# Two attention and mixer layers on one core: the order in which the last V and the weights are loaded at a layer's end, and what PE does meanwhile

## The chip, the core and the metric

The kernel runs on one core of a Trainium2 chip. The metric is the device time of one execution in microseconds (us). Before the change it is 2575.71 us, the median of three runs (2574.78 to 2576.16). Times "at 1268" are microseconds from the start of the profiled execution's span.

## What is computed

A decode step of two layers for a batch of two rows of 576 values. Each layer does, in this order:

```
x = x + attention(layernorm(x)) @ wo        # 32 heads of 128, 16384 cached positions, per row
x = x + B(layernorm(x))                     # a mixer: h = gelu(layernorm(x) @ w1), shifted along
                                            # the sequence, @ w2; then gelu(layernorm(x1) @ w3) @ w4
attention: q = x @ wq;  p = softmax(q . K * 128**-0.5);  o = p @ V
```

Both layers use the same weights and the same K and V caches. One row's head (here a *unit*; there are 64, unit u is head u // 2 of row u % 2) has a K of 16384 x 128 bf16 values, 4096 KB, and a V of the same size. The sequence is one token long, so the shifted h is zero wherever it would be used, and w1 and w2 are loaded and multiplied all the same.

## The kernel before, in words

**What is where.** One SBUF array `mem` holds everything that is loaded: an area at its start (`AUX`, 6144 bytes of each partition), which during attention holds three buffers `kt` for transposed K, and behind it six slots of 32768 bytes, each as large as one K or V tile. `Store` (L250) keeps account of it. `plan_all` (L469) writes down by hand, in order, every load with its place: `plan_tile` for K and V, `plan_cols` for wq and w3 (128 rows of the matrix a piece, the last piece the remaining 64 rows), `plan_heads` for wo, `plan_groups` for w4, `plan_small` for w1 and w2. `Store.pump` (L271) issues the loads strictly in that order, all on SP's queue: a load is issued as soon as every cell of its place is free, and one whose place isn't free holds all those behind it. `used` and `release` free a place behind the instruction that reads it last.

**A step of attention** (`attention`, L859 and on). For each unit, half of K's blocks are transposed by PE in chunks of eight blocks (`transposes`, L1012) into a PSUM buffer `tps` (four of them), copied by ACT to `kt` (`evacuate`, L1022) and multiplied with q by PE (`scores`, L1032). The other half goes to DVE, as a product with a broadcast q and a sum (`dots`, L1047 and L1051, four pairs a unit). `softmax_max` (L1058 and on) takes maxima, with a GpSimd reduction over partitions; `softmax_exp` (L1073 and on) takes exponentials on ACT; `pv` (L1103) multiplies with V, one step later, in four quarters. So V of unit s is used in the step of unit s + 1.

**Order of the units.** Layer 0 goes from unit 0 to 63. Layer 1 begins with 62, 63, 61, 60, because the K of units 61 to 63 and the V of units 62 and 63 are still in their slots (`held`) and aren't loaded again; then it goes from 0 to 59. In layer 1 the two kept heads 62 and 63 have 40 instead of 32 of each half's 64 blocks transposed (`PB_KEPT`), and the first four chunks are transposed ahead of wq (`early_transposes`).

**The end of attention** (`last_head`). While the last unit's V is still to come, the sums of all other units are formed (`total`, L937), o is normalised, and wo is multiplied for all heads but the last (`heads_projection`, `rows_step`, L794). wo comes as head rows: for `a` to `b` heads, partition p of the piece gets row p of each head, 1152 bytes a run. In the plan, wo stands ahead of the last unit's V, which comes in four parts; in layer 0 wo's last pieces lie in AUX, which is free only when the last scores are done.

**Behind it**: `two_norms` gives the mixer's inputs, then w3 (`cols_projection`, L730 and L740), `gelu` (L828 to L833), w4 in eight groups (`groups_projection`, L794 again), the next layer's `input_norm`, and wq (`q_projection`). Weights of layer 0's end go into AUX and into slot 0, the only places that are free while five slots hold kept tiles; so a piece of w3 waits until a piece of wo has been multiplied, w4 until w3 has, wq until w4 has, and the next K tile until wq has. In layer 1 nothing is kept, and all weights find free slots.

Of the kernel before, what the change touches and what calls it, by code (L numbers as in the profile page):

```python
# [5 lines left out]
ALU = mybir.AluOpType  # L6
# [306 lines left out]
class KB:  # L313
# [12 lines left out]
    PB_KEPT = 40  # L326
    GROUPS = (6, 6, 6, 6, 6, 3, 2, 1)

    def __init__(self, nc, A_x, K, V, wq, wo, w1, w2, w3, w4, out):
# [20 lines left out]
        self.chunk = 0  # L350
# [4 lines left out]
    def _alloc(self):  # L355
# [21 lines left out]
        self.otn = sb("otn", [128, U], BF16)  # L377
        n = 2 * MT * B
# [3 lines left out]
        self.linv = self.prod[:, 512:512 + 2 * U].bitcast(FP32)  # L382
        self.linv_last = self.prod[:, 640:642].bitcast(FP32)
# [46 lines left out]
    def plan_cols(self, nm, l, w, ats):  # L430

        n = w.shape[1]
        for k, at in ats:
            if k < self.KT - 1:
                self.store.plan((nm, l, k), f"{nm}{k}", at, 2 * n, [(lambda m: m, w[k * 128:(k + 1) * 128, :])])
            else:
                self.store.plan((nm, l, k), f"{nm}{k}", at, n,
                                [(lambda m: m, w[k * 128:, :].rearrange("r (h n) -> (r h) n", h=2))])
        self.korder[nm, l] = [k for k, _ in ats]

    def plan_heads(self, l, cuts):

        D = self.D
        self.cuts["wo", l] = [(a, b) for a, b, _ in cuts]
        for i, (a, b, at) in enumerate(cuts):
            self.store.plan(("wo", l, i), f"wo{i}", at, 2 * (b - a) * D, [
                (lambda m: m.rearrange("p (j n) -> p j n", n=D),
                 self.wo[a * 128:b * 128, :].rearrange("(j p) n -> p j n", p=128))])
# [20 lines left out]
    def plan_all(self):  # L469
# [11 lines left out]
        for i, (t, u) in enumerate(tiles[:-1]):  # L481
            self.plan_tile(source[t], t, u, place[i])
            if i == 0:
                self.store.plan(None, "xin", 0, 0, [(self.rows[0:B, :], self.A_x.rearrange("b s d -> (b s) d"))], ["prod"])
                self.plan_cols("wq", 0, self.wq, [(k, s[0] + wqr * k) for k in range(self.KT)])
                self.plan_small("w2", 0, self.w2, s[0] + wqr * (self.KT - 1) + wqr // 2, (0, 64))
        at = s[0]
        self.plan_heads(0, [(0, 11, at), (11, 21, at + 11 * row), (21, 28, at + 21 * row), (28, 31, 0), (31, 32, 3 * row)])
        rest = self.store.queue[-2:]
        del self.store.queue[-2:]  # L490
        self.plan_tile(self.V, *tiles[-1], place[-1], 4)
        self.store.queue[-2:-2] = rest
        at = 4 * row
        self.plan_cols("w3", 0, self.w3, [(0, at), (1, at + w3r), (2, at + 2 * w3r), (4, at + 3 * w3r), (3, 0)])
        self.plan_groups(0, [w3r, w3r + g[0], w3r + g[0] + g[1], w3r + g[0] + g[1] + g[2], 0, g[4], g[4] + g[5],
                             g[4] + g[5] + g[6]])
# [696 lines left out]
```

## Time and profile before

| | |
|---|---|
| median of three runs | 2575.71 us |
| the profiled execution's own time | 2575.98 us |
| its span, first to last instruction | 2574.2 us |
| busy: PE, DVE, ACT, GpSimd | 63%, 73%, 47%, 6% |
| read from HBM | 1094.21 MB, 425 GB/s over the span |
| mean granted TensorE clock | 0.572 |

How to read it: the page's section 2 cuts the span in 40 equal slices of 64.4 us and gives each engine's busy tenths, the granted clock, the share of time in which the 16 DMA engines are busy, and GB/s. The stretches of the trace give the same for any window. In the chain, a line "DMA mem<-in_A_wo_dram" is the time from a transfer's issue to its landing, as far as something waited for it. A transfer's issue is an instruction of SP (SPq L98).

### The profile page before, as it was taken

The numbers are of one execution on the slowest core, as the hardware profiler recorded it, in microseconds if no ns is written. First come the engines' busy times: TensorE is split into PE (matmuls) and PEld (weight loads), VectorE is DVE, ScalarE is ACT, GpSimd is POOL, SyncE is SP. The second block draws the span as 40 slices with busy tenths as digits, with TensorE's granted clock in tenths as the row PEclk, the third lists the DMA queues.
The fourth block names the chain that finished last, engine by engine and source line by source line (L and its number), as shares of the span: only waits on it lengthen the run. The fifth ranks groups of instructions, "written<-read, shape, count | busy, mean of one in ns | idle before, by whom it ended". The sixth has DMA issues, their size and how long they took to land.

```text
span 2574.2 us, 73686 instructions
## 1 busy us (share of the span) xinstructions
PE 1623.4 (63%) x34362; PEld 1587.6 (62%) x34362; DVE 1889.8 (73%) x1905; ACT 1208.0 (47%) x1822; POOL 160.0 (6%) x151
## 2 busy tenths in 40 slices
PE   4766566666666656666667766666665665666565
PEld 3666566566656656666567766665665665666565
DVE  5877777776777777777549977777777777777773
ACT  3544444444544444454335554454444444445442
POOL 0000000000000000000000000000000000000000
PEclk8555655555555555555555655555555556555555
DMA  9999999999999999999999999999999999999998
GB/s 409 431 432 432 431 432 432 432 431 432 431 432 432 431 432 432 431 432 432 359 365 425 433 431 432 431 431 432 432 431 432 431 432 432 431 432 431 432 431 357
DMA packets 52143, 1095.27 MB, mean 425 GB/s; under 512 B 4954, under 2 KB 14558, under 8 KB 16862
## 3 DMA queue, kind: packets, MB, share of 16 engines
q1 hardware_dynamic: 52062, 1094.23, 99.4%
q8 instruction: 46, 0.75, 0.1%
q14 instruction: 35, 0.29, 0.0%
HBM read 1094.21 MB, written 0.00 MB: 425 GB/s over the span
## 4 chain that ended last, share of the span: by engine, by line
DMA 64%; DVE 28%; PE 5%; issue 1%; SPq 1%; ACT 0%; POOL 0%; another core or an unknown queue 0%; DVEq 0%; POOLq 0%
DMA mem<-in_A_k_cache_dram 61%; DVE s_dve L1051 17%; DVE prod L1047 9%; DMA mem<-in_B_w_dram 3%; PE tps L1012 2%; PE mps L1103 2%; SPq L98 1%; PE sps L974 1%; DMA mem<-in_A_wq_dram 0%; DMA mem<-in_A_wo_dram 0%; DVE diag L971 0%; DVE mx L1062 0%; DVE mx L1060 0%; DVE mx L1058 0%; PE sps L794 0%
## 5 line engine op out<-in xcount | busy, mean ns | idle before, releaser
L1022 ACT ACTIVATE mem<-tps 128x1024 bf16<-128x1024 bf16 x1028 | 1038.3, 1023 | 868.6 <-PE tps L1012 851.7
L1051 DVE TENSOR_REDUCE s_dve<-prod 128x16 f32<-128x2048 bf16 (+1 forms) x512 | 1166.1, 2278 | 17.5
L1012 PE MATMUL tps<-ident,mem 128*128 128x128 bf16 x8224 | 1004.9, 300 | 172.4 <-POOLq L177 171.0
L1047 DVE TENSOR_TENSOR prod<-mem,qb 128x2048 bf16<-128x2048 bf16 (+1 forms) x512 | 624.1, 1219 | 538.0 <-DMA mem<-in_A_k_cache_dram 520.6
L1103 PE MATMUL mps<-p,mem 128*128 128x1 bf16 x16384 | 515.6, 166 | 596.3 <-ACT p L1078 521.8
L1012 PEld LDWEIGHTS tps<-ident,mem 128*128 128x128 bf16 x8224 | 766.1, 136 | 181.8 <-POOLq L177 180.8
L1103 PEld LDWEIGHTS mps<-p,mem 128*128 128x128 bf16 x16384 | 487.7, 105 | 607.4 <-ACT p L1078 599.2
L1032 PEld LDWEIGHTS sps<-q_col,mem 128*128 128x128 bf16 x8224 | 413.2, 113 | 4.8 <-ACT mem L1022 4.7
L1032 PE MATMUL sps<-q_col,mem 128*128 128x1 bf16 x8224 | 401.5, 170 | 4.1 <-ACT mem L1022 4.1
L1065 POOL PARTITION_ALL_REDUCE mx<-mx x128 | 157.7, 1232 | 2358.8 <-DVE mx L1062 2358.8
L1073 ACT ACTIVATE mx<-mx 128x1 f32<-128x1 f32 x128 | 25.9, 203 | 325.9 <-POOL mx L1065 325.9
L974 PE MATMUL sps<-diag,ones_bf 128*128 128x128 bf16 x128 | 36.8, 288 | 119.6 <-DVE diag L971 119.6
L974 PEld LDWEIGHTS sps<-diag,ones_bf 128*128 128x128 bf16 x128 | 13.3, 104 | 130.4 <-DVE diag L971 130.4
L977 ACT ACTIVATE qb<-sps 128x128 bf16<-128x128 f32 x128 | 35.4, 277 | 75.2 <-PE sps L974 75.2
L1075 ACT ACTIVATE p<-s_dve,mx 128x64 bf16<-128x64 f32 x128 | 44.5, 348 | 4.2
L1078 ACT ACTIVATE p<-sps,mx 128x64 bf16<-128x64 f32 x128 | 37.5, 293 | 0.0
L1060 DVE TENSOR_REDUCE mx<-sps 128x1 f32<-128x64 f32 x128 | 27.4, 214 | 10.0 <-PE sps L1032 10.0
L559 ACT ACTIVATE sc<-sc 128x2 f32<-128x2 f32 x8 | 1.6, 204 | 65.5 <-DVE sc L556 65.5
L971 DVE TENSOR_SCALAR diag<-ident,q_f 128x128 bf16<-128x128 bf16 x128 | 31.3, 245 | 0.3 <-PE sps L974 0.3
L1058 DVE TENSOR_REDUCE mx<-s_dve 128x1 f32<-128x64 f32 x128 | 26.7, 208 | 0.1
L730 PE MATMUL sps<-xn,mem 128*128 128x2 bf16 x544 | 21.0, 174 | 9.1 <-DMA mem<-in_A_wq_dram 6.6
L730 PEld LDWEIGHTS sps<-xn,mem 128*128 128x128 bf16 x544 | 20.2, 122 | 9.6 <-DMA mem<-in_A_wq_dram 7.0
(96 smaller groups left out, 214.3 us busy)
## 6 DMA issues: line engine op xcount, KB each, us to landing
mem<-in_A_k_cache_dram SPq DMA_DIRECT2D x124, 4096.0 KB, 41.2
mem<-in_A_v_cache_dram SPq DMA_DIRECT2D x123, 4096.0 KB, 49.9
mem<-in_B_w_dram SPq DMA_DIRECT2D x8, 1152.0 KB, 15.7
mem<-in_B_w_dram SPq DMA_DIRECT2D x10, 864.0 KB, 17.7
mem<-in_A_wq_dram SPq DMA_DIRECT2D x8, 1024.0 KB, 12.4
mem<-in_A_v_cache_dram SPq DMA_DIRECT2D x8, 1024.0 KB, 10.7
mem<-in_A_k_cache_dram SPq DMA_DIRECT2D x2, 2048.0 KB, 9.2
mem<-in_A_v_cache_dram SPq DMA_DIRECT2D x2, 2048.0 KB, 9.6
```

Of the source, the lines that this page charges most:

```text
L730: ins = pe.matmul(out[:, m * B:(m + 1) * B], lhsT=buf[:, c:c + 127 * d + 1:d], rhs=self.xn[:, k, :], start=first and m == 0, stop=False, s ...
L974: self.pe(lambda pe: pe.matmul(qps, lhsT=self.ones_bf[:, :], rhs=self.diag[:, :], start=True, stop=True, skip_group_check=True), reads=["o ...
L977: self.act(lambda e: e.activation(out=self.qb[s % 2][:, :], in_=qps, func=ACT.Copy), reads=[("qps", i)], writes=[("qb", s % 2)])
L1012: ins = pe.transpose(self.tps[t][:, j * 128:(j + 1) * 128], buf[:, j * 128:(j + 1) * 128], self.ident[:, :])
L1022: self.act(lambda e: e.activation(out=self.kt[k], in_=self.tps[t][:, :].rearrange("p (i c) -> p i c", i=self.CH), func=ACT.Copy), reads=[( ...
L1032: ins = pe.matmul(self.sps[sp][:, c * self.CH + j:c * self.CH + j + 1], lhsT=self.kt[k][:, j, :], rhs=self.q_col[:, sp:sp + 1], start=True ...
L1047: self.dv(lambda e: e.tensor_tensor(out=prod, in0=buf.rearrange("p (j d) -> p j d", d=128), in1=qbc, op=ALU.mult), reads=[("qb", s % 2)] + ...
L1051: self.dv(lambda e: e.tensor_reduce(out=sd[:, c0:c0 + DB], in_=prod, axis=AX.X, op=ALU.add), reads=["prod"], writes=[("s_dve", s % 2)])
L1065: self.pool(lambda e: e.partition_all_reduce(self.mx[:, 3, m:m + 1], self.mx[:, 2, m:m + 1], channels=128, reduce_op=ROP.max), reads=[("mx ...
L1075: self.act(lambda e: e.activation(out=p[:, n:self.NB], in_=self.s_dve[s % 2][:, 0:self.NB - n], func=ACT.Exp, bias=self.mx[:, 4, m:m + 1], ...
L1078: self.act(lambda e: e.activation(out=p[:, 0:n], in_=self.sps[i][:, 0:n], func=ACT.Exp, bias=self.mx[:, 4, m:m + 1], scale=self.scale, acc ...
L1103: ins = pe.matmul(self.mps[:, 448:449], lhsT=buf[:, j * 128:(j + 1) * 128], rhs=p[:, col:col + 1], start=(h == 0 and b == 0), stop=(h == 1 ...
```

## The change

1. **Order of the loads.** In both layers the last unit's V is planned as one tile ahead of wo, in its turn as every other tile. In layer 1 the slots' ring is `[0, 5, 1, 2, 4, 3]` instead of `[0, 5, 2, 1, 4, 3]`, and the first tile (K of unit 60) comes in four parts, in the order 1, 2, 3, 0.
2. **wo's shape.** wo comes in five pieces: three of eight heads (1024 rows of the matrix), and the last eight heads cut in two. Partition p of such a piece gets the eight rows 8p to 8p + 7, one run of 9216 bytes. To match, o must lie so that partition p holds those rows' values: `dealt` multiplies the normalised o with eight selections of the identity's columns (`every`, copied by DVE), masks the product and sums it, for the first 48 units (`oA`) and later for the last 16 (`oB`). wo's pieces 0 to 2 use `oA`, the last eight heads `oB`; all are multiplied behind the last unit's PV.
3. **w3, w4, wq of layer 0's end** have new places in AUX and slot 0; w3's piece 3 comes in two halves; wq's order is 1, 2, 3, 4, 0.
4. **Both kept K** are transposed in full, in place: `ahead` has PE transpose a chunk into a `tps` buffer, `lay` has ACT copy it back to where it came from. Their 32 chunks are strewn between the sums, the pieces of wo, the norms, w3, w4 and wq. In layer 1 `kept_heads` scores units 62 and 63 straight from the transposed K, all 128 blocks on PE and none on DVE, both heads one after the other, before the loop over the other units begins.
5. **Small ones.** `touch` runs one-element activations to have a table loaded earlier; keys of the `prod` scratch are split.

The core of the diff:

```diff
     def plan_heads(self, l, ats):
+        cuts = [(i, 0, hg) for i in range(self.ng - 1)] + [(self.ng - 1, 0, self.WO_CUT), (self.ng - 1, self.WO_CUT, hg)]
+        for i, ((a, lo, hi), at) in enumerate(zip(cuts, ats)):
+            src = self.wo[a * hg * 128:(a + 1) * hg * 128, :].rearrange("(p j) n -> p (j n)", j=hg)
+            self.store.plan(("wo", l, i), f"wo{i}", at, 2 * (hi - lo) * D, [(lambda m: m, src[:, lo * D:hi * D])])
...
-        for i, (t, u) in enumerate(tiles[:-1]):
+        for i, (t, u) in enumerate(tiles):
             self.plan_tile(source[t], t, u, place[i])
...
-        self.plan_heads(0, [(0, 11, at), (11, 21, at + 11 * row), (21, 28, at + 21 * row), (28, 31, 0), (31, 32, 3 * row)])
-        self.plan_tile(self.V, *tiles[-1], place[-1], 4)
+        self.plan_heads(0, [a, a + r8, a + 2 * r8, 0, a + 3 * r8])
+        self.plan_cols("w3", 0, self.w3, [full(0, mt, a), full(1, mt, a + w3r), full(2, mt, a + 2 * w3r),
+                                          full(4, mt, a + 3 * w3r), (3, 0, mt // 2, 0), (3, mt // 2, mt, a)])
...
+    def ahead(self, l, n):
+        for _ in range(n):
...
+            nm, buf, keys = self.chunk_of(c)
+            def f(pe, buf=buf, t=t):
+                for j in range(self.CH):
+                    ins = pe.transpose(self.tps[t][:, j * 128:(j + 1) * 128], buf[:, j * 128:(j + 1) * 128],
+                                       self.ident[:, :])
...
+    def lay(self, l, n):
...
+            self.act(lambda e, buf=buf, t=t: e.activation(out=buf, in_=self.tps[t][:, :], func=ACT.Copy),
+                     reads=[("tps", t)], writes=keys)
...
+    def kept_heads(self, l, o):
+        for c in range(n):
+            self.kept_scores(l, 0, o[0], c)
+        self.softmax_max(l, 0, o[0])
+        while self.laid or self.made < 2 * n:
+            self.lay(0, 1)
+            self.ahead(0, 1)
+        for c in range(n):
+            self.kept_scores(l, 1, o[1], c)
+        self.softmax_exp(l, 0, o[0])
+        self.softmax_max(l, 1, o[1])
+        for g in range(4):
+            self.pv(l, 0, o[0], g)
+        self.keep_o(0, o[0])
+        self.softmax_exp(l, 1, o[1])
+        for g in range(4):
+            self.pv(l, 1, o[1], g)
...
     def last_head(self, l, s, u, before):
+        self.shares(0, late)
+        self.normed(0, late)
+        self.ahead(l, 2)
+        self.dealt(0, late, self.sps[2], ("sps", 2), self.masked[0], self.oA[:, :], "oA")
+        self.ahead(l, 2)
+        self.lay(l, 2)
+        self.softmax_exp(l, s, u)
+        self.touch(ACT.Sqrt)
+        self.lay(l, 2)
+        self.shares(late, U)
+        for g in range(4):
+            self.pv(l, s, u, g)
+        self.keep_o(s, u)
+        self.normed(late, U)
+        self.heads_projection(l, 0)
+        self.ahead(l, 1)
+        self.dealt(late, U, self.sps[0], ("sps", 0), self.masked[1], self.oB[:, :], "oB")
+        for i in range(1, len(self.cuts["wo", l])):
+            self.heads_projection(l, i)
+            if i < 3:
+                self.ahead(l, 2)
+                self.lay(l, 2)
+        self.lay(l, 4)
```

Further fillers (`ahead`) stand behind the statistics of `two_norms` (2) and of the next `input_norm` (2), ahead of w3's last half piece (3), behind each w4 group but the first (1 each) and behind each wq piece but the last (1 each).

More of the change, by code (lines that the diff above doesn't have):

```diff
@@ L325 @@
     PB = 32
-    PB_KEPT = 40
+    HG = 8
+    WO_CUT = 5
+    PK = ["prod", "gT", "hf", "every"]
     GROUPS = (6, 6, 6, 6, 6, 3, 2, 1)
@@ L745, in cols_projection @@
             first = False
+            if w == "w3" and i == len(order) - 2:
+                self.ahead(l, 3)
+                self.lay(l, 2)
+            if w == "wq" and i < len(order) - 1:
+                self.ahead(1 - l, 1)
+                self.lay(1 - l, 1)
     def q_projection(self, l):
@@ L941, in last_head @@
[L941 to L949 removed]
+        i, hg = self.ident[:, :], self.HG
```

339 lines of the change are left out of this document (201 added, 138 removed).

## The prediction

> **What bounds the kernel now.** I read the page's slices first, then its chain, then stretches of the trace around the turn from layer 0 to layer 1, then the chain in that stretch.
>
> ```profile
> span 2574.2 us, 73686 instructions
> PE   4766566666666656666667766666665665666565
> DMA  9999999999999999999999999999999999999998
> GB/s 409 431 432 432 431 432 432 432 431 432 431 432 432 431 432 432 431 432 432 359 365 425 433 431 432 431 431 432 432 431 432 431 432 432 431 432 431 432 431 357
> DMA 64%; DVE 28%; PE 5%; issue 1%; SPq 1%; ACT 0%; POOL 0%; another core or an unknown queue 0%; DVEq 0%; POOLq 0%
> ```
>
> The DMA engines are busy in every slice and move 431 to 433 GB/s in all but five: the first, three at the layer turn and the last. The kernel is a stream of bytes; only stretches in which the stream thins can be won back. One 4096 KB tile at 432 GB/s takes 9.71 us. Inside the turn (start:end, width, busy time of PE, PEld, DVE, ACT, POOL, granted clock, DMA share, GB/s):
>
> ```profile
> 120.00:1200.00 1080.00, 673.42 (x14151) 659.82 (x14149) 811.49 (x778) 513.67 (x777) 70.17 (x56) 0.57 1.00 432
> 1250.00:1260.00 10.00, 5.45 (x97) 5.37 (x96) 9.83 (x10) 6.05 (x10) 1.25 (x1) 0.67 0.77 273
> 1260.00:1270.00 10.00, 9.09 (x236) 8.90 (x234) 5.45 (x9) 5.29 (x9) 0.35 (x1) 0.50 1.04 383
> 1270.00:1280.00 10.00, 4.96 (x152) 4.80 (x150) 0.17 (x1) 0.00 (x0) 0.00 (x0) 0.50 0.56 194
> 1280.00:1290.00 10.00, 3.66 (x99) 3.22 (x96) 1.46 (x10) 0.06 (x1) 0.00 (x0) 0.50 1.01 426
> 1290.00:1300.00 10.00, 6.74 (x152) 6.66 (x153) 2.30 (x16) 0.35 (x2) 0.00 (x0) 0.50 0.77 288
> 1340.00:1350.00 10.00, 9.07 (x213) 8.99 (x211) 9.54 (x9) 6.21 (x11) 0.00 (x0) 0.50 0.63 236
> ```
>
> The stream thins where wo is issued (1250), where the queue runs dry behind wo (1270), behind w3 (1290), and at the first tiles of layer 1 (1340). The chain of waits, and then the issue of the transfers, say why (start, duration):
>
> ```profile
> 1245.08 15.85 SPq L98 DMA_DIRECT2D mem<-in_A_wo_dram  x2
> 1266.68 8.79 DMA mem<-in_A_wo_dram
> 1277.57 9.75 DMA mem<-in_B_w_dram
> 1287.46 0.28 PE sps L794 x5
> 1291.91 1.57 PE sps L730 x36
> 1293.50 5.61 DMA mem<-in_B_w_dram
> 1313.73 10.89 DMA mem<-in_A_wq_dram
> ```
>
> SP stands 15.85 us in issuing two wo pieces, and the last V waits behind them in SP's order. Three heads of wo wait for the kt buffers until 1266.68, the last head waits until those have landed, and half of the last V waits for that.
>
> **Before, in landings.** Each of these transfers is alone in a narrow stretch of the DMA view (KB, us from issue to landing): V of unit 62, issued at 1208.1; layer 1's K of unit 3, issued at 1401.9; V of unit 58, issued at 2470.99:
>
> ```profile
> mem<-in_A_v_cache_dram SPq DMA_DIRECT2D x1, 4096.0 KB, 51.0
> mem<-in_A_k_cache_dram SPq DMA_DIRECT2D x1, 4096.0 KB, 17.7
> mem<-in_A_v_cache_dram SPq DMA_DIRECT2D x1, 4096.0 KB, 51.1
> ```
>
> They land at 1259.1, 1419.6 and 2522.1. Between the first two come wo and wq (4.72 MB each), w3 and w4 (5.31 each) and ten tiles (41.9 MB): 62.0 MB, 143.5 us at 432 GB/s, where 160.5 passed. So 17 us can be won at the turn, and that is the ceiling.
>
> **The change, by a walk along the turn.** Durations for it (timeline; two pieces of the chain; three groups of the page):
>
> ```profile
> 1266.51 1.09 PE L937 MATMUL sps<-l,mean_f 128*128 128x63 f32 x4
> 1268.52 2.74 PE L794 MATMUL sps<-otn,mem 128*128 128x2 bf16 x97 [0.91 <-DVE otn L552]
> 1268.56 1.28 ACT L559 ACT_TABLE_LOAD   x1
> 1278.88 2.98 PE L1103 MATMUL mps<-p,mem 128*128 128x1 bf16 x96
> 1291.78 4.82 PE L730 MATMUL sps<-xn,mem 128*128 128x2 bf16 x108
> 1313.37 0.36 DVE L549 TENSOR_TENSOR st<-st,mps 128x8 f32<-128x8 f32 x2 [6.80 <-PE mps L794]
> 1313.98 0.62 PE L626 MATMUL mps<-st,mean_f 128*128 128x20 f32 x2 [0.65 <-DVE st L549]
> 1314.43 3.58 PE L1012 MATMUL tps<-ident,mem 128*128 128x128 bf16 x32
> 1317.81 0.24 PE L701 MATMUL mps<-xn,sel 128*128 128x2 bf16 x2
> 1258.64 0.44 ACT p L1075 x2
> 1259.08 0.30 ACT p L1078 x2
> L1022 ACT ACTIVATE mem<-tps 128x1024 bf16<-128x1024 bf16 x1028 | 1038.3, 1023 | 868.6 <-PE tps L1012 851.7
> L1051 DVE TENSOR_REDUCE s_dve<-prod 128x16 f32<-128x2048 bf16 (+1 forms) x512 | 1166.1, 2278 | 17.5
> L1047 DVE TENSOR_TENSOR prod<-mem,qb 128x2048 bf16<-128x2048 bf16 (+1 forms) x512 | 624.1, 1219 | 538.0 <-DMA mem<-in_A_k_cache_dram 520.6
> ```
>
> So a weight step of wo, w4 or wq costs 0.028 us a matmul (40 of them 1.15), one of w3 0.045 (36: 1.6), a filler of eight transposes 0.9 on PE and its copy back into K 1.02 on ACT, a quarter of PV 0.9.
>
> *1. V ahead of wo.* V63 now waits in SP's order for V60's slot only, freed one step (two tiles, 19.4 us) after the issue of V62: 1227.6, so wo behind it isn't held. It lands one tile after V62, at 1268.8, in one piece. wo follows from the other slot, where its issue was (1242.7 to 1247), in 9216-byte rows like w3's, so at 426 instead of 383 GB/s: 11.1 us, front at 1279.9. The queue has work throughout, and the 15.85 us of issuing goes, since a piece has 128 rows of one run instead of 1408.
>
> *2. First hand-over, w3's piece 0 into wo's piece 0.* PE: scores end 1266.5; sums 1.1; two fillers 1.8 (1269.4); eight dealing matmuls; two fillers (to 1271.8); sums again 1.0; PV of V63 3.5 (1276.3); 40 matmuls: w3 is issued at 1277.4. The trace shows no dealing matmul of 48 columns: between 8 x 0.028 = 0.2 and 8 x 0.11 (a transpose, 128 columns) = 0.9; I take 0.6, the nearer of them. DVE's copy of `every` (1024 elements, 0.6 to 1.2 by the rows of 2048), the masked product and its sum lie beside fillers and PV; uncovered they would cost some 2 us. On ACT two copies stand ahead of the last exponential and end at 1270.6; with 0.74 for the exponentials and 0.2 for the scale they still make PE's second sums at 1271.8.
>
> What an issue into a short queue costs is in the row of 1293.50: 5.61 us for 1152 KB, of which 2.8 at 426 GB/s, so 2.8 more. [...] Landing is then 1283.0 instead of 1282.7: **0.3 lost**. The next pieces are issued at 1280.2, 1283.1 and 1286.1 (each 1.15 behind one or two fillers, and once the dealing); the last of these is a 576 KB one, landing at 1286.1 + 2.8 + 1.4 = 1290.3 instead of 1289.9: **0.4 lost**. The front is at 1291.7 with all of w3 but its last 576 KB.
>
> *3. Second hand-over, w3's last half piece.* It needs piece 0 consumed. From the end of wo's matmuls to w3's first took 1287.74 to 1291.91 = 4.2; the fillers there sit beside DVE's norm. So 1286.1 + 4.2 + 1.6 = 1291.9, issue; landing 1291.9 + 2.8 + 1.4 = 1296.1 where a full queue had 1293.1: **3.0 lost**. w4 follows without a gap (pieces issued 1293.4, 1295, 1296; three fillers, 2.65, delay its fifth to 1300.4, still 5 us before its turn): 12.5 us, 1308.6. The sigmoid's table load of 1.28 leaves the path; that only hides fillers, as w4 is ahead.
>
> *4. Third hand-over, layer 1's first K into wq.* w4's eight steps end at 1313.3 with a filler each, as before (1313.37, the row of the x update), so the norm starts no earlier, though wq now lands at 1319.7 instead of 1313.73 + 10.89 = 1324.6. After the last w4 step PE runs a filler (0.9), the statistics (0.6), two fillers (1.8) and the spreading (0.24): wq's first step is at 1316.9, and the second is done at 1319.7 (0.9, a filler, 0.9): issue, landing of the 1024 KB at 1325.0 where a full queue had 1322.1: **2.9 lost**. The other three parts: 1332.4. wq is done at 1324.7.
>
> *5. Kept heads.* 128 score matmuls (3.5) free unit 62's slot at 1329.5; V61 lands at 1343.1, allowing 3.8 instead of 2.8 for a tile (**1.0 lost**). Five leftover fillers follow on PE, and ACT's five copies behind the first of them (1330.4) end at 1335.5, the second head's scores at 1337.4, its PV at 1344.5: two more slots, all earlier than their turn. DVE idles meanwhile and starts unit 61 at 1344.8; with four products of 1.22 + 2.28 a step takes 15.6, and each slot still comes free 1 to 5 us before its turn. K of unit 3 lands seven tiles after V61: 1411.1. **Gain 8.5.**
>
> *6. The end.* In layer 1 the order is V59, wo, w1, w3, w4, each into slots free some 10 us before. The last of it before:
>
> ```profile
> 2549.13 21.13 DMA mem<-in_B_w_dram
> 2570.31 0.67 PE mps L794 x15
> ```
>
> From 2522.1 to 2570.3 stands 48.2; V59 at 432 and wo, w3, w4 (15.34 MB) at 426 GB/s need 9.7 + 36.0 = 45.7. **Gain 2.5.** The tail behind the last w4 group, the start and the steady steps are as before; three GpSimd instructions more at the start lie under the first K.
>
> **Sum.** 8.5 + 2.5 = 11.0 from the profiled execution's 2575.98 us (span 2574.2 and 1.8 around it): 2565.0; the median stands 0.3 below that execution: **2564.7**. A difference under 0.2% (5.2 us) is about what a measurement can't tell from none.
>
> **Rivals.**
>
> *No thin places left (0.10).* The 7.6 us lost in steps 2 to 5 don't appear: 2557.1. What would do it is a faster PE on the filled stretch. The clock after a stretch full of transposes:
>
> ```profile
> 1329.90:1333.30 3.40, 3.40 (x53) 3.40 (x51) 3.30 (x4) 3.40 (x5) 0.00 (x0) 0.50 1.03 434
> 1333.30:1336.70 3.40, 2.27 (x60) 2.09 (x59) 3.33 (x3) 3.10 (x4) 0.00 (x0) 1.00 0.99 414
> ```
>
> Full clock was granted there. If it held from 1270 on, each filler would cost half (0.45), PE would be 4 us early at step 3 and more at step 4. Against it stands the row of 1260, 91% busy with PV and transposes mixed and granted 0.50; the new stretch is such a mixture. [...]
>
> *The gain is handed back (0.14).* The front's lead is worth something only if PE keeps pace, and steps 3 and 4 show that the chain is no earlier than before. If each of the four hand-overs is 2 us later than I walked it (semaphore steps, the deal at 0.9, ACT's queue), 8 more go: 2572.7, within 0.2%.
>
> *Slower (0.08): ACT sets the fillers' pace.* Four transpose buffers separate PE from ACT. If ACT, which runs copies, exponentials and three table loads in one order, falls four behind, a filler costs PE its 0.9 plus the copy's 1.02 and the hand-shake, about 1.1 more. Over the 23 fillers between 1277 and 1325 that is 25 us on the chain that issues w3, w4, wq and the first K; the queue's spare time in w4 takes about 6: 2584, from 0.75 us more a filler on it is slower than before. Against it: a filler comes every 1.2 to 1.9 us in these stages, and ACT needs 1.02.
>
> That the change doesn't do what it says could only be if V63's issue were still held; it waits for one slot, freed in a step that exists already (under 0.01).
>
> **Chances.** Forecast 0.68 (2560 to 2569), the others 0.10, 0.14, 0.08. Range 2558 to 2572.5: down to nearly all of the first rival, up over half of the second; the dealing, the copies and the tile's 2.8 or 3.8 lie inside it. Faster 0.78, within 0.2% 0.14, slower 0.08.
>
> **What would show it.** Step 1: no thin stretch between 1250 and 1277, V63 landed by 1269, and no long issue of wo. Steps 2 to 4: GB/s dips near 1292 to 1295 and 1321 to 1323, each under 4 us; a missing one speaks for the first rival, wide ones with PE waiting for ACT's copies for the third. Step 5: K of unit 3 landed near 1411. Step 6: over 420 GB/s from 2495 to the last w4. I am wrong if the fillers wait for ACT, or if layer 1's first steps hold their slots past their turn.

## The result, and the profile after

After the change the kernel takes 2567.69 us (median of 9 runs, 2566.81 to 2568.81), before it 2575.71 us: ratio 0.997, 95% interval 0.996 to 0.998. The forecast was 2564.7, with a range of 2558 to 2572.5. The profiled execution took 2568.3 us.

From the page of the changed kernel:

```profile
span 2566.6 us, 74123 instructions
GB/s 409 431 432 432 430 431 432 433 432 432 431 432 431 433 432 432 432 432 432 387 396 415 431 431 432 432 432 430 432 431 433 431 433 431 430 433 432 432 430 360
DMA 64%; DVE 28%; PE 6%; issue 2%; ACT 0%; SPq 0%; POOL 0%; another core or an unknown queue 0%; DVEq 0%; POOLq 0%
```

The three slices at the turn read 387, 396 and 415 where they read 359, 365 and 425, and SP's queue, 1% of the chain before, is at 0. Stretches of the turn, with two (1310 and 1370) that the prediction didn't show (start:end, width, busy time of PE, PEld, DVE, ACT, POOL, granted clock, DMA share, GB/s):

```profile
1250.00:1260.00 10.00, 4.96 (x94) 4.87 (x93) 9.83 (x10) 5.93 (x10) 1.25 (x1) 0.67 0.99 423
1260.00:1270.00 10.00, 10.00 (x214) 10.00 (x212) 6.67 (x11) 4.49 (x5) 1.18 (x1) 0.50 0.97 399
1270.00:1280.00 10.00, 9.64 (x258) 9.47 (x256) 2.03 (x7) 6.25 (x12) 0.00 (x0) 0.67 0.56 209
1290.00:1300.00 10.00, 8.62 (x176) 8.54 (x176) 0.81 (x5) 4.22 (x6) 0.00 (x0) 0.61 0.87 298
1310.00:1320.00 10.00, 8.38 (x197) 7.72 (x195) 1.55 (x10) 7.74 (x10) 0.00 (x0) 0.92 1.02 423
1340.00:1350.00 10.00, 7.82 (x206) 7.68 (x204) 3.08 (x5) 2.08 (x3) 0.00 (x0) 0.50 1.03 439
1370.00:1380.00 10.00, 6.79 (x173) 6.71 (x174) 9.17 (x8) 4.01 (x9) 1.24 (x1) 0.50 0.83 356
```

Two thin places are gone, at 1250 (273 to 423 GB/s) and at 1340 (236 to 439). Those at 1270 (194 to 209) and 1290 (288 to 298) stay, and one has come at 1370, where the prediction had none (the kernel before moved 437 GB/s there and was thin ten microseconds later, 392 GB/s from 1380 to 1390). SP's timeline has the issues around them (start, duration). The DMA view of one narrow stretch for each gives, in the same order, their sizes and the us from issue to landing. They are w3's last half piece and w4's first piece, then V of unit 61 and K of units 2 and 3 (V61, K2 and K3 from here on):

```profile
1289.84 0.33 SPq L98 DMA_DIRECT2D mem<-in_B_w_dram  x1
1291.41 0.33 SPq L98 DMA_DIRECT2D mem<-in_B_w_dram  x1
1327.14 0.33 SPq L98 DMA_DIRECT2D mem<-in_A_v_cache_dram  x1
1379.24 0.33 SPq L98 DMA_DIRECT2D mem<-in_A_k_cache_dram  x1
1394.83 0.33 SPq L98 DMA_DIRECT2D mem<-in_A_k_cache_dram  x1
```

```profile
mem<-in_B_w_dram SPq DMA_DIRECT2D x1, 576.0 KB, 4.4
mem<-in_B_w_dram SPq DMA_DIRECT2D x1, 864.0 KB, 7.4
mem<-in_A_v_cache_dram SPq DMA_DIRECT2D x1, 4096.0 KB, 14.9
mem<-in_A_k_cache_dram SPq DMA_DIRECT2D x1, 4096.0 KB, 13.6
mem<-in_A_k_cache_dram SPq DMA_DIRECT2D x1, 4096.0 KB, 17.5
```

V61 landed at 1342.1, K2 at 1392.8, K3 at 1412.3. K3 lies seven tiles behind V61, which at 9.71 us would have been 1410.0: 2.3 us were lost between them, nearly all in front of K2, whose slot came free only at 1379.24: K2 landed 11.9 us behind the tile ahead of it (V of unit 0, 1380.9). In the kernel before K3 landed at 1419.6, so the turn gained 7.3.

The place of K2 is slot 0, which holds the K of unit 60. What SP waited for there (times in us: total, count, longest):

```profile
SPq L98 <- PE tps L1133: 16.0, 1, 16.0
```

That is TensorE's last transposes of unit 60 (they end at 1379.20). In TensorE's order they stand behind the broadcast of the next q, and VectorE prepares that only when it is done with unit 60's dot products, which stand behind unit 61's. From 1347.1 to 1376.9 VectorE works without a pause of over 0.7 us. So K2's slot is late because VectorE begins unit 61 late. VectorE of the changed kernel, from the end of the kept heads (start, duration, idle time before it and what ended that):

```profile
1341.15 0.16 DVE L1225 COPY o_acc<-mps 128x1 f32<-128x1 f32 x1 [6.20 <-PE mps L1244]
...
1347.05 0.16 DVE L1225 COPY o_acc<-mps 128x1 f32<-128x1 f32 x1 [5.73 <-PE mps L1244]
1347.12 1.22 DVE L1181 TENSOR_TENSOR prod<-mem,qb 128x2048 bf16<-128x2048 bf16 x1
```

It has next to nothing to do during the two PV of the kept heads, and since its order is fixed, unit 61's products start only behind the copy of the second one's result. TensorE at that place:

```profile
1334.48 1.44 PE L1244 MATMUL mps<-p,mem 128*128 128x1 bf16 x51
1338.92 2.20 PE L1244 MATMUL mps<-p,mem 128*128 128x1 bf16 x77 [3.00 <-issue]
1341.46 1.50 PE L1244 MATMUL mps<-p,mem 128*128 128x1 bf16 x51 [0.34 <-DVE o_acc L1225]
1344.80 2.21 PE L1244 MATMUL mps<-p,mem 128*128 128x1 bf16 x77 [1.84 <-issue]
```

Both PV stop after 51 of 128 matmuls, for 3.00 and 1.84 us, with no releaser that the profile knows. Without the gaps each would take 3.6 us (1.44 and 2.20).

### The profile page after: what moved, and what is told of

It is laid out like the page before. It is cut to its first block, busy times and chain, and to the rows that moved or that the text cites. A ratio compares the mean times of both kernels' runs of the same rounds, so it can differ in the third digit from the quotient of the medians.

```text
span 2566.6 us, 74123 instructions
## 1 busy us (share of the span) xinstructions
PE 1631.5 (64%) x34584; PEld 1596.3 (62%) x34584; DVE 1873.2 (73%) x1897; ACT 1219.3 (48%) x1832; POOL 161.1 (6%) x154
## 4 chain that ended last, share of the span: by engine, by line
DMA 64%; DVE 28%; PE 6%; issue 2%; ACT 0%; SPq 0%; POOL 0%; another core or an unknown queue 0%; DVEq 0%; POOLq 0%
DMA mem<-in_A_k_cache_dram 61%; DVE s_dve L1185 17%; DVE prod L1181 9%; DMA mem<-in_B_w_dram 2%; PE mps L1244 2%; PE tps L1133 2%; PE sps L1095 1%; PE tps L660 1%; DMA mem<-in_A_wq_dram 0%; PE sps L869 0%; DVE diag L1092 0%; DVE mx L1200 0%; PE sps L801 0%; DVE mx L1197 0%; PE sps L1165 0%
## 5 line engine op out<-in xcount | busy, mean ns | idle before, releaser
L1143 ACT ACTIVATE mem<-tps 128x1024 bf16<-128x1024 bf16 x1008 | 1019.1, 1023 | 868.7 <-PE tps L1133 851.9
L1185 DVE TENSOR_REDUCE s_dve<-prod 128x16 f32<-128x2048 bf16 x504 | 1152.1, 2286 | 17.3
L1181 DVE TENSOR_TENSOR prod<-mem,qb 128x2048 bf16<-128x2048 bf16 x504 | 616.5, 1223 | 538.0 <-DMA mem<-in_A_k_cache_dram 520.8
L1133 PEld LDWEIGHTS tps<-ident,mem 128*128 128x128 bf16 x8064 | 750.7, 136 | 181.6 <-POOLq L177 180.2
L1153 PEld LDWEIGHTS sps<-q_col,mem 128*128 128x128 bf16 x8064 | 406.3, 113 | 0.3 <-ACT mem L1143 0.3
L1153 PE MATMUL sps<-q_col,mem 128*128 128x1 bf16 x8064 | 394.0, 170 | 0.1
L678 ACT ACTIVATE mem<-tps 128x1024 bf16<-128x1024 bf16 x32 | 30.9, 1022 | 16.5 <-PE tps L660 16.4
L1225 DVE COPY o_acc<-mps 128x1 f32<-128x1 f32 x128 | 19.0, 148 | 18.1 <-PE mps L1244 18.1
```

Source lines behind the costliest of these rows:

```text
L1133: ins = pe.transpose(self.tps[t][:, j * 128:(j + 1) * 128], buf[:, j * 128:(j + 1) * 128], self.ident[:, :])
L1143: self.act(lambda e: e.activation(out=self.kt[k], in_=self.tps[t][:, :].rearrange("p (i c) -> p i c", i=self.CH), func=ACT.Copy), reads=[( ...
L1153: ins = pe.matmul(self.sps[sp][:, c * self.CH + j:c * self.CH + j + 1], lhsT=self.kt[k][:, j, :], rhs=self.q_col[:, sp:sp + 1], start=True ...
L1181: self.dv(lambda e: e.tensor_tensor(out=prod, in0=buf.rearrange("p (j d) -> p j d", d=128), in1=qbc, op=ALU.mult), reads=[("qb", s % 2)] + ...
L1185: self.dv(lambda e: e.tensor_reduce(out=sd[:, c0:c0 + DB], in_=prod, axis=AX.X, op=ALU.add), reads=["prod"], writes=[("s_dve", s % 2)])
```

## The experiments

The theory from the two traces: **at the turn, the front of transfers is held by two things in turn**, first by the hand-overs of the weights, where TensorE's chain decides, and then by K2's slot, which comes free as VectorE gets through units 61 and 60. What the front gains ahead of K2 counts only as far as that slot lets it. The rival: transfers alone set the turn, and a microsecond gained anywhere is one gained at the end. Times of all runs, with three events of each trace (us):

| kernel | V61 landed | K2 issued | K3 landed | time, median | ratio to before, 95% |
|---|---|---|---|---|---|
| before | 1345.7 (two parts) | 1386.3 | 1419.6 | 2575.71 | |
| changed | 1342.1 | 1379.2 | 1412.3 | 2567.69 | 0.996 to 0.998 |
| V behind wo | 1348.9 | 1385.5 | 1418.9 | 2573.07 | 0.9981 to 0.9999 |
| wo as head rows | 1342.9 | 1380.1 | 1413.2 | 2568.79 | 0.9961 to 0.9983 |
| dots early | 1340.4 | 1371.5 | 1409.7 | 2565.21 | 0.9944 to 0.9971 |
| w1 behind w3 | 1340.7 | 1379.3 | 1412.2 | 2568.47 | 0.9959 to 0.9981 |
| fillers early | 1338.2 | 1378.1 | 1411.2 | 2567.06 | 0.9952 to 0.9979 |
| dots and fillers early | 1337.8 | 1369.5 | 1407.3 | 2563.46 | 0.9939 to 0.9966 |
| fillers late | 1347.5 | 1392.6 | 1425.6 | 2581.61 | 1.0015 to 1.0033 |
| old kept heads | 1341.8 | 1378.7 | 1414.1 | 2569.06 | 0.9965 to 0.9984 |
| both early, spaced | 1339.3 | 1372.7 | 1407.9 | 2563.35 | 0.9937 to 0.997 |

The intervals are 5 to 9 us wide. The single runs of "wo as head rows", "w1 behind w3", "fillers early" and "old kept heads" overlap with those of the changed kernel (2566.81 to 2568.81); those of the others don't. Where a difference of 1 to 2 us is used below, it is because the events of the traces go along with it.

**V behind wo.** Only layer 0's last V goes back.

```diff
+        last_v = self.store.queue.pop()
...
         self.plan_heads(0, [a, a + r8, a + 2 * r8, 0, a + 3 * r8])
+        self.store.queue.insert(len(self.store.queue) - 2, last_v)
```

> The changed kernel, with layer 0's last V tile planned behind the first three pieces of layer 0's wo instead of ahead of them; everything else, wo's rows of eight heads and the kept K included, stays. Theory: what the place of V is worth is the wait of wo's first matmuls, which stand behind the last unit's PV on TensorE. V63 then lands at about 1277 us in place of 1268.9 (wo's three pieces of 1152 KB pass first, some 8 us), the last PV, the deal of o and wo's matmuls start that much later, w3's first issue falls from 1276.4 to about 1281.6, and the front of transfers runs dry there: some 5 us over the changed kernel, about 2572.5 us, most of the change's gain gone. Rival: the shape of wo's rows brought the gain and V's place is hidden: within 1 us of the changed kernel, about 2568 us.

Measured 2573.07, 5.4 over the changed kernel. The chain of waits of this run, and its stretch at 1270:

```profile
1247.50 29.66 DMA mem<-in_A_v_cache_dram
```

```profile
1270.00:1280.00 10.00, 4.67 (x127) 4.41 (x125) 1.37 (x3) 5.08 (x11) 0.00 (x0) 0.67 0.30 123
```

V63 landed at 1277.16. PV waited for it, and behind PV all of wo, so the queue had nothing to do (123 GB/s). V's place in layer 0 is worth 5.4 of the 8.0 us, through the order on TensorE.

**wo as head rows.** V stays ahead; wo comes in 1152-byte runs and o isn't dealt out.

```diff
-            src = self.wo[a * hg * 128:(a + 1) * hg * 128, :].rearrange("(p j) n -> p (j n)", j=hg)
+            src = self.wo[(a * hg + lo) * 128:(a * hg + hi) * 128, :].rearrange("(j p) n -> p j n", p=128)
...
-        self.dealt(0, late, self.sps[2], ("sps", 2), self.masked[0], self.oA[:, :], "oA")
```

> The changed kernel, with V ahead of wo, but wo taken as rows of one head (1152-byte runs, 1024 of them in a piece, as in the kernel before) and o not dealt out; the kept K stay. Theory: the shape is worth little: pieces of 1152-byte runs pass at about 383 GB/s instead of 432, so the front lands about 1.1 us later in layer 0, against which the deal's 0.4 to 0.5 us on the way to w3 is saved: 0 to +1.5 us over the changed kernel, 2567.7 to 2569.2 us; SP has one long issue again. Rival: the shape matters, because 1024 descriptors in a piece hold SP's queue at the end of layer 1 or at the first hand-over: +3 us or more, 2571 us and over.

Measured 2568.79, 1.1 more (inside the spread of the runs); V61, K2 and K3 are 0.8 to 0.9 later. SP's timeline shows the hold:

```profile
1242.69 31.23 SPq L98 DMA_DIRECT2D mem<-in_A_wo_dram  x5
```

SP spends 31 us on wo's pieces, and it costs next to nothing, because V63 was issued ahead of them and nothing urgent stands behind. So it was not the 15.85 us of issuing by themselves that hurt before, but that the last V stood behind them.

**Dots early.** VectorE's idle stretch within the kept heads is used for unit 61's dot products.

```diff
-                if c % n in (0, 2):
+                if c % n in (0, 2) and not (l and s == base):
                     self.dots(l, s, u, h, c % n // 2)
...
+        self.dots(l, 2, o[2], 0, 0)
         self.softmax_max(l, 0, o[0])
+        self.dots(l, 2, o[2], 0, 1)
+        self.dots(l, 2, o[2], 1, 0)
...
         self.softmax_max(l, 1, o[1])
+        self.dots(l, 2, o[2], 1, 1)
```

> The changed kernel, with the four dot products of layer 1's unit 61 (the third slot of the kept heads) issued on VectorE within the kept heads, where it idles from 1322 to 1347 us, instead of in the loop's first steps. Theory: K2's slot is handed on late because VectorE starts unit 61's dots only at 1347, so K2 lands at 1392.8 where its 9.7 us behind V0 would give 1390.6; with the dots early it lands on time and the whole stream behind it about 2 us earlier: about 2565.6 us. The gaps of TensorE within the kept heads (3.0 and 1.84 us at 1335.9 and 1343) stay. Rival: the slot waits for TensorE, held by its gaps, and not for VectorE: 0, about 2567.7 us.

Measured 2565.21, 2.5 under the changed kernel. SP's timeline, and the stretch that was thin:

```profile
1371.52 0.33 SPq L98 DMA_DIRECT2D mem<-in_A_k_cache_dram  x1
```

```profile
1370.00:1380.00 10.00, 6.44 (x126) 6.35 (x124) 8.73 (x9) 3.86 (x5) 1.06 (x1) 0.50 1.00 427
```

K2 is issued 7.7 us earlier and the thin place is gone (356 to 427 GB/s). TensorE's gaps in the two PV are still there (2.85 and 1.84 us), so the slot waited for VectorE. Of the 2.7 us at K3, though, 1.7 are there at V61 already, ahead of the edit: executions differ by 1 to 2 us in how late w4's first piece lands (1298.8 in the changed kernel, 1297.4 here, 1296.7 in the next run, with the same program up to there). What this run alone can't tell, the next two do.

**w1 behind w3**, in layer 1's plan.

```diff
-        self.plan_small("w1", 1, self.w1, a, (0, 56, 64))
+        w1_at = a
         a += row * self.KT
...
+        self.plan_small("w1", 1, self.w1, w1_at, (0, 56, 64))
```

> The changed kernel, with layer 1's w1 planned behind w3 instead of ahead of it; no other edit. Theory: the issue of w1's second part holds SP for 30.9 us (2492.7 to 2523.6) and V58, V59 and wo behind it are issued late and land 0.94 and 0.3 us late; moved behind w3 the hold falls where the ring has no slot free anyway: 1 to 1.5 us off, about 2566.5 us. Rival: only the bytes count at the end and the hold hides behind transfers already issued: 0, about 2567.7 us; w1's users may even wait for it, +1 us.

Measured 2568.47: the theory of SP's hold falls. V58 takes 50.8 us from issue to landing in both kernels, whether w1 stands ahead of w3 or behind it:

```profile
mem<-in_A_v_cache_dram SPq DMA_DIRECT2D x1, 4096.0 KB, 50.8
```

But this run brought something else. By chance V61 landed 1.4 us earlier than in the changed kernel (1340.7, the spread just named), and yet:

```profile
1379.27 0.33 SPq L98 DMA_DIRECT2D mem<-in_A_k_cache_dram  x1
```

K2 was issued at the same time to 0.03 us, and K3 landed at 1412.2, only 0.1 earlier. The lead was lost at K2's slot.

**Fillers early**, without the dots' edit.

```diff
                     if c == n:
+                        if s == U - 1:
+                            self.ahead(l, 3)
+                            self.lay(l, 2)
                         self.softmax_exp(l, s - 1, o[s - 1])
+                        if s == U - 1:
+                            self.lay(l, 1)
...
-        self.ahead(l, 2)
+        self.ahead(l, 1)
         self.dealt(0, late, self.sps[2], ("sps", 2), self.masked[0], self.oA[:, :], "oA")
-        self.ahead(l, 2)
-        self.lay(l, 2)
+        self.ahead(l, 1)
...
         self.heads_projection(l, 0)
-        self.ahead(l, 1)
...
             if i < 3:
-                self.ahead(l, 2)
-                self.lay(l, 2)
+                self.ahead(l, 1)
+                self.lay(l, 1)
```

> The changed kernel with its fillers (the transposes of the kept K and their copies back) placed otherwise: three of them, of unit 62's K, go into the step of unit 63 where TensorE waits from 1254.5 to 1259.5 us for the exponentials; in return the last head has 1, 1, 0, 1, 1 where it had 2, 2, 1, 2, 2, and two more are left for the kept heads. The slots of layer 1's unit 61 are handed on as in the changed kernel. Theory: the hand-overs into w3's last half piece and w4 come some 4 us earlier, so the front of transfers is 3 to 4 us ahead at wq and V61; but K2's slot, which in the changed kernel and in the run with w1 behind w3 was issued at 1379.24 and 1379.27 although V61 had landed 1.4 us apart, sets the turn's end, and moves only with the chain on TensorE and VectorE (1 to 2 us): 2566 to 2567.5 us. Rival: transfers set the turn's end throughout, and the 3 to 4 us are kept to the end: about 2564 us.

Measured 2567.06, 0.6 less. SP's timeline, V61 and K2:

```profile
1324.88 0.33 SPq L98 DMA_DIRECT2D mem<-in_A_v_cache_dram  x1
...
1378.06 0.33 SPq L98 DMA_DIRECT2D mem<-in_A_k_cache_dram  x1
```

V61 landed 3.9 us earlier, K3 1.1. The thin place at K2 took the rest: K2 landed 13.8 us behind the tile ahead of it, where 9.71 would do.

**Both edits**, the dots and the fillers early.

> Both edits: the fillers placed early as in the run before, and unit 61's four dot products issued within the kept heads, so that K2's slot is free some 8 us ahead of its turn. Theory: nothing stands behind the front of transfers then, and what the early fillers gain at the hand-overs (3 to 4 us) is kept: 3 us under the run with the dots early alone (2565.2 us), about 2562 us. Rival: the hand-overs' losses are the queue's own (pieces land late however early they are issued): within 1 us of it, 2564.5 to 2565.5 us.

Measured 2563.46, 4.2 under the changed kernel and 12 under the kernel before, and with "both early, spaced" (2563.35) the best version here. SP's timeline:

```profile
1369.54 0.33 SPq L98 DMA_DIRECT2D mem<-in_A_k_cache_dram  x1
```

Now K3 is 5.1 us ahead of the changed kernel, where the fillers alone gave 1.1 and the dots alone 2.7. Against the run with the dots alone the gain is 1.8 by the medians and 2.4 at K3, not 3. The theory stands: of the 3.9 us gained at V61 by the early fillers, 1.1 were left behind the held slot; once the slot is early, the 2.6 us that V61 leads are kept to 0.2.

**Fillers late**: none among the weights, all 32 within the kept heads.

```diff
-        if l:
+        if l or not self.kept:
             return
...
+        self.kept = True
+        for c in range(n):
+            self.ahead(0, 1)
+            self.lay(0, 1)
         for c in range(n):
             self.kept_scores(l, 0, o[0], c)
```

> The changed kernel with no filler while weights pass: all 32 chunks of the kept K are transposed within the kept heads, the first head's 16 ahead of its scores, the second head's 16 behind them. Theory: the hand-overs into w3's last half piece, w4, and layer 1's first K come 3 to 8 us earlier than in the changed kernel, but 16 copies of 1.02 us on ScalarE stand ahead of the first head's scores and five fillers become sixteen ahead of the second's, so that V61's slot is free some 10 us later and the next two some 15; the stream stands still before V61 and K0: about 8 us over the changed kernel, 2576 us, no gain over the kernel before. Rival: the fillers among the weights are what costs the hand-overs, and the kept heads have the time: under 2567 us.

Measured 2581.61: the direction was right, the price too low by 5.6. Stretches of this run:

```profile
1320.00:1330.00 10.00, 8.33 (x104) 7.13 (x101) 0.00 (x0) 10.00 (x13) 0.00 (x0) 0.85 0.42 172
1330.00:1340.00 10.00, 9.70 (x192) 9.62 (x193) 0.30 (x2) 8.66 (x11) 0.35 (x1) 0.67 0.54 208
1340.00:1350.00 10.00, 8.33 (x195) 7.21 (x193) 0.00 (x0) 10.00 (x12) 0.00 (x0) 0.99 0.51 217
```

ScalarE is busy for 8.7 to 10 of each 10 us with the copies, and the stream runs at half. The expectation took what the hand-overs gain (the last part of layer 1's first K landed 5.9 us earlier) off what the slots lose. But a slot's time doesn't depend on how early its turn comes; the lead was lost here too, and K3 is 13.3 late.

**Old kept heads**: the changed loads, with the kept heads of the kernel before and no fillers.

```diff
+        pre = self.early_transposes(l)
         self.q_projection(l)
...
     def ahead(self, l, n):
...
-        if l:
-            return
+        return
...
-        return self.BP if l and s < self.CARRY else self.PB
+        return self.PB_KEPT if self.kept(l, s) else self.PB
...
-        if l:
-            self.kept_heads(l, o)
-        else:
-            self.q_broadcast(o[0], 0)
+        for s in range(2 if l else 1):
+            self.q_broadcast(o[s], s)
...
-        ring = [0, 5, 1, 2, 4, 3]
+        ring = [0, 5, 2, 1, 4, 3]
```

> The changed kernel with its loads, its wo and its deal of o, but with the kept heads as in the kernel before: nothing is transposed while weights pass or in place, the kept K goes through the kt buffers within the kept heads, 40 of each 64 blocks by TensorE and the rest as dot products on VectorE. Theory: K2's slot sets the turn's end. In the kernel before it was issued 60.3 us after q was there (1326.0 to 1386.26), in the changed one 56.9 us (1322.38 to 1379.24); without fillers wq lands some 4.5 us earlier than in the changed kernel (1316.1 in the run with the fillers late, q there at 1317.9), so K2 is issued at about 1378 and the end is within 1.5 us of the changed kernel: 2566 to 2569 us. So the transposing in place bought 3.4 us in the kept heads and paid about as much at the hand-overs. Rival: transposing while weights pass is what won the turn: 2571 us or more, as the run with the fillers late (2581.6 us) lets one think.

Measured 2569.06, 1.4 over the changed kernel, just past the top of the theory's range (2569) and below the rival's (2571). SP's timeline, then two pieces of the chain:

```profile
1378.68 0.33 SPq L98 DMA_DIRECT2D mem<-in_A_k_cache_dram  x1
```

```profile
1378.84 0.85 PE mps L1252 x32
1379.70 7.02 issue
```

K2 is issued 0.6 us earlier than in the changed kernel. What it then loses is a gap of 7.02 us on TensorE of the same kind as those in the kept heads, behind which K3's slot is late. So transposing in place by itself is worth nothing up to K2, and at most 1.4 us with the gap, which lies inside the spread of the runs; as it stands in the changed kernel it isn't what won the turn.

**Both early, spaced**: the run with both edits, and 32 transposes of the identity ahead of the first PV. What are the gaps put down to "issue"?

```diff
+        t = self.chunk % self.NT
...
+        def f(pe):
+            for j in range(4 * self.CH):
+                i = j % self.CH
+                ins = pe.transpose(self.tps[t][:, i * 128:(i + 1) * 128], self.ident[:, :], self.ident[:, :])
+            return ins
+        self.pe(f, reads=["ident"], writes=[("tps", t)])
         for g in range(4):
             self.pv(l, 0, o[0], g)
```

> The run with both edits (2563.5 us), with 32 transposes of the identity more (into a transpose buffer that nobody reads, about 3.4 us of TensorE) ahead of the first kept head's PV. It asks what TensorE's gaps in the kept heads are. There both PV stop after 51 of their 128 matmuls, for 2.33 us (until 1336.45) and 2.11 us (until 1342.60), with the gap put down to issue; from one gap to the next lie 77 + 51 = 128 matmuls. Theory: the supply of instructions. The gaps stand at fixed places of the program and end when the next block of it arrives, whatever TensorE did meanwhile. The first gap's place then comes 32 matmuls earlier, after 19 of the PV, the added 3.4 us fill it and it shrinks under 0.5 us; the second comes after 19 of its PV too and still ends at about 1342.6; the second PV ends some 1 us later than without the addition (1344.8), at about 1345.7. Rival: a wait of the PV itself (for data or a buffer that the profile doesn't show): the gaps stay after 51 matmuls with some 2 us each and the second PV ends 3.4 us later, at 1348.2. By both the time stays at 2563 to 2564.5 us, since the slots behind have that much to spare.

Measured 2563.35. TensorE's timeline of this run:

```profile
1332.86 3.18 PE L1045 MATMUL tps<-ident 128*128 128x128 bf16 x32
1335.88 3.59 PE L1259 MATMUL mps<-p,mem 128*128 128x1 bf16 x128
1339.81 0.65 PE L1259 MATMUL mps<-p,mem 128*128 128x1 bf16 x19 [0.34 <-DVE o_acc L1240]
1343.31 3.07 PE L1259 MATMUL mps<-p,mem 128*128 128x1 bf16 x109 [2.85 <-issue]
```

The first gap is gone: 128 matmuls in 3.59 us without a stop. The second moved from 51 to 19 matmuls into its PV, by the 32 that were added, and the second PV ends 1.6 us later than without them (1346.4 and 1344.8), where 3.2 us of work were added; nearer the theory's 1 than the rival's 3.4, and 0.2 us of it stood there before the added work began (1332.86 and 1332.62). The gaps stand at fixed places of the program and end at a time of their own (the second at 1342.60 without the added work and at 1343.31 with it); they are no wait of the PV.

## Why the prediction was right, and where it was not

The mechanism was right, and the sum too high by 3: 11.0 expected, 8.0 measured (7.7 between the two profiled executions). That it came this near is in part luck, since steps 3 and 4 below missed in opposite directions. By its steps:

1. *V ahead of wo: right.* V63 was expected at 1268.8 and landed at 1268.9; the front behind wo came at 1279.9 as expected; no long issue of wo is left. The runs give V's place 5.4 us and wo's rows 1.1. One sign that I named was wrong, though: between 1270 and 1280 the queue is thin (209 GB/s, share 0.56). wo's landings keep their pace there, 8.2 us for the 3456 KB of its first three pieces from V63's landing on (430 GB/s). But the bytes run out ahead of the landings: in the single microseconds from 1274 to 1277 the DMA share is 0.13, 0.11 and 0.05, two engines of 16 or one, while wo's last piece lands at 1279.9 and w3 is issued at 1276.4. So "the queue has work throughout" was wrong, though the landings don't show it.
2. *First hand-over: right.* The front with all of w3 but its last 576 KB was expected at 1291.7 and came at 1291.6, though w3 was issued 1 us earlier than walked (1276.4 instead of 1277.4).
3. *Second hand-over: near in size, not in place.* 3.0 us were to be lost in w3's last half piece, and w4 was to follow without a gap. The half piece was issued at 1289.8, two us earlier than walked, and lost 1.2 (landed at 1294.3); but w4's first piece, issued at 1291.41 with that half piece still in flight, took 7.4 us to land (1298.8) and lost 2.5, so 3.7 in all. w4 was through at 1309.6 instead of 1308.6.
4. *Third hand-over: wrong.* 2.9 us were to be lost at the first part of layer 1's first K. That part lost nothing: it landed at 1323.0, 2.4 us behind wq's last piece. All four parts were through 11.3 us behind wq (1331.9), 1.6 more than their bytes need, of which 1.3 are in the last part; in the nine other runs with the new loads that part lost nothing (2.4 to 2.5 us behind the third, here 3.7), so this is a spread between executions. The first part was issued at 1316.5 instead of 1319.7. 1.6 of these 3.2 us were there when w4's steps ended (1311.7 instead of 1313.3). The others go with the row of 1310, 0.92 of the clock granted and 423 GB/s: from 1312.7 on the fillers took about half the 0.9 us that I gave each (the first two 1.05 us together). A faster clock is what the rival "no thin places left" said of this place. That rival took the clock for the whole stretch, and the rows of 1260, 1270 and 1290 have 0.50 to 0.67. Busy time alone doesn't give the clock in these rows: in the row of 1260 PE is busy for all of its 10 us and has 0.50, in 1310 it is busy for 8.38 and has 0.92.
5. *Kept heads: the step that failed.* "Each slot still comes free 1 to 5 us before its turn" held for every slot but K2's. I had unit 61's products start at 1344.8; they started at 1347.1, because the two PV took 12.5 us (1334.5 to 1347.0) with 4.8 us of gaps in them, where the walk had 7.1. The slot came free at 1379.24, 1.7 us ahead of the landing before it (1380.9). By the 3.8 us that I had allowed, an estimate, for a tile that starts behind an emptying queue (13.6 us from issue to landing here, 3.9 over its 9.71) it had to be 3.8 us ahead. Cost: 2.2 us at K2. V61 itself was 1 us better than expected. Gain at the turn 7.3 instead of 8.5; with the dots early, 9.9 in the profiled execution, 1.7 of it from V61's earlier landing in that execution.
6. *The end: a term left out.* 2.5 us were to be won behind V59. From the landing of unit 59's K to the last matmuls of w4 the rows are, in the changed kernel (SP's timeline, the DMA view, the chain):

```profile
2463.03 0.33 SPq L98 DMA_DIRECT2D mem<-in_A_k_cache_dram  x1
```

```profile
mem<-in_A_k_cache_dram SPq DMA_DIRECT2D x1, 4096.0 KB, 41.2
```

```profile
2539.46 23.23 DMA mem<-in_B_w_dram
2562.74 0.64 PE mps L869 x15
```

K59 landed at 2504.2, and w4's last matmuls began 58.5 us later. In the kernel before it landed at 2511.15 and they began at 2570.31: 59.2. Gain 0.7. The 45.7 us that I set against 48.2 counted V59, wo, w3 and w4 and forgot w1, which passes in the same stretch: 576 rows of 1152 bytes, 0.66 MB, 1.6 us at 426 GB/s. Its time shows in the landings: w3's first piece, behind w1, landed 4.5 us after wo's last, where its own bytes need 2.8; with w1 behind w3 it landed 2.8 us after, and w4's first piece, now behind w1, 3.9 us after w3's last, where 2.1 would do. With w1 the step gives 0.9. What is won there is wo's rows: in the run with head rows the last piece of w4 landed 59.4 us behind K59, in the kernel before 59.5, in the changed kernel 58.8. The sign that I named, over 420 GB/s from 2495 on, failed too: 416 GB/s from 2500 to 2530 and 385 from 2530 to 2560.

So of the 3 us, 1.2 are K2's slot net of the better hand-overs, and 1.8 the end, 1.6 of them the forgotten w1.

*The rivals:* "handed back" (2572.7) was wrong as a sum, and right in one thing, that a lead is worth only what the chain behind it can use (of 3.9 us at V61 the early fillers kept 1.1). "ScalarE sets the fillers' pace" is refuted by the groups of the page (busy, mean ns of one, idle time before and its releaser):

```profile
L678 ACT ACTIVATE mem<-tps 128x1024 bf16<-128x1024 bf16 x32 | 30.9, 1022 | 16.5 <-PE tps L660 16.4
...
L660 PE MATMUL tps<-ident,mem 128*128 128x128 bf16 x256 | 27.5, 288 | 1.0 <-issue 1.0
```

ScalarE's copies wait 16.4 us for the transposes, and the transposes wait for ScalarE not at all. It is the other way round only where they come without weights between them, in the run with the fillers late (there a chunk waits 0.30 us for a copy to end, from 1325 on).

## What to carry to other kernels

Where a stream is held by one thing after another, find the last one that holds it: a gain ahead of it shows in every landing up to there and not in the end (with w1 behind w3, 1.4 us at V61 and 0.1 at K3). Before a slot is called early, walk the engine that frees it through its whole order, since an idle engine with its work queued behind a foreign result is as late as a busy one (VectorE stood idle for 5.73 us until the second PV's result came, and began unit 61 at 1347.1). And list every transfer of a stretch before its bytes are summed.

## What the runs showed of the hardware

- **In the kept heads TensorE stops at fixed places of the program, and the stops end behind instruction packets.** In the changed kernel's two PV the stops are 128 one-column matmuls (with their 128 weight loads) apart, 77 + 51; the spaced run shows that the place is the program's and that work put ahead of it hides the gap. In the DMA view of 1317.6 to 1349.8 of the changed kernel stands:

```profile
q8 instruction: 5, 0.08, 1.0%
```

Five packets of 16 KB in 32 us, of some 1 us each. The traces' records of these packets show what the ends of the gaps go along with. In the changed kernel two packets end at 1337.6 and 1343.5, and the gaps in the two PV end at 1338.9 and 1344.8, each 1.3 us later. In the traces of the changed kernel and of the nine runs, 27 gaps of 0.8 us or more on TensorE, in the kept heads and the steps next to them, are put down to "issue" (the 7.02 us of the old kept heads among them), and every one ends 1.2 to 1.6 us behind the end of such a packet. The four of the changed kernel end at 1320.06, 1325.98, 1338.92 and 1344.80, and the packets ahead of them at 1318.43, 1324.71, 1337.58 and 1343.48. Why a packet comes as late as it does stays open.
- **w4's first piece, behind a short queue, was up to 2.5 us late, by a spread.** Its 864 KB took 7.4 us in the changed kernel; issued 3.3 us earlier in the run with the fillers early, it took 6.4 us and landed 2.5 behind the piece before it, of which 2.1 are its bytes. An issue into an empty queue is seen in the run with V behind wo, w3's first piece, issued at 1281.9 when the front had ended at 1280:

```profile
mem<-in_B_w_dram SPq DMA_DIRECT2D x1, 1152.0 KB, 5.3
```

2.8 us of it are the bytes at 426 GB/s, and 2.5 are over; I had taken 2.8.

How far an issue stands ahead of the landing before it explains part of the spread. For w4's first piece, 4.7 or 4.8 us ahead lost nothing (fillers late, old kept heads), 3.8 to 4.0 lost 0.4 to 1.1 (fillers early, both early, spaced), and 2.1 to 2.9 lost 0.9 to 2.5 (the others). For K2, 3.3, 2.8, 2.2, 1.7 and 0.8 us ahead lost 0.6, 1.4, 1.5, 2.2 and 2.8 (old kept heads, before, V behind wo, changed, w1 behind w3); 1.7 lost 1.8 in the run with head rows. What makes the rest, up to 1.1 us at K2 with 8 us of lead (dots early), stays open.
